# Splitting the next expert's weights into second buffers, two pieces a job over three jobs, in a mixture-of-experts loop on one core

## The chip, the cores and the metric

The kernel runs on one core of one Trainium2 chip. The metric is device time in microseconds (us); lower is better. The engines are named as in the profile: PE is TensorE (PEld its weight loads), DVE is VectorE, ACT is ScalarE, POOL is GpSimd, SP is SyncE, which issues most DMAs. Each engine runs its own instruction stream and waits for others on semaphores. A name with a q (ACTq) is the sequencer that feeds an engine: it executes branches and register work and hands out the instructions.

## The reference

Two stages. The first is a linear attention with decay over 32 pairs of batch and head:

```
for t in range(S):                                   # S = 768, head_dim 48
    cur = einsum('bhd,bhe->bhde', u * kt, vt)
    y[:, :, t] = einsum('bhd,bhde->bhe', rt, state + cur)
    state = w * state + einsum('bhd,bhe->bhde', kt, vt)
```

Its output, as 3072 tokens of 384 numbers, goes through a mixture of eight experts, one expert per token:

```
logits = x @ w_gate + modality_bias[modality_id]
e_idx, gate_w = argmax(logits), softmax(logits)[e_idx]
for e in range(8):
    h = maximum(x[e_idx == e] @ w1[e], 0.0)          # w1: 384 x 1024
    out[e_idx == e] = gate_w * (h @ w2[e])           # w2: 1024 x 384
```

## The kernel before, in words

**The stages.** Up to about 204 us of the profile the attention runs in 24 units of 128 tokens, and each unit's tokens are sent to rows of a buffer in memory sorted by expert. Beside the attention the first nine jobs of the first expert are worked off. A *job* is 128 rows of one expert. For this data three experts get tokens: 1569, 1354 and 149.

**The job table.** When the counts are known, DVE computes a table on the device (`jobs`) with a column per remaining job: the row to start from (ROW), a code (CODE) and the number of an expert to load (MORE). There are 17 such jobs here: 4 of the first expert, 11 of the second, 2 of the third. Job 0 is written out ahead of a hardware loop (`For_i`), whose 16 turns work off jobs 1 to 16. So the expert changes at job 4 and at job 15.

**One job.** `raise_` multiplies the job's tokens (`mxT`, held as a high and a low f16 half) by w1 into `phb`, in three groups of 4, 2 and 2 blocks of 128 columns (g0, g1, g2). ACT takes the relu of each group into `hh` (f16, the high half), DVE the rest into `hl`. `high_terms` multiplies `hh` by w2's high and low halves into `po`, `low_terms` multiplies `hl` by the high half; `low_terms` and `put` of a job stand at the top of the next turn. `put` has ACT scale `po` by the gate's factor `fac` into `otb`, and POOL send `otb` out by an indirect DMA. `take_in` has DVE copy the next job's tokens from `xn`, where a DMA has put them, to `mxT`, and their gates from `mn` to `mt`.

**The weights.** An expert's w1 and w2 lie as 6144 columns of 32-bit numbers per partition in `raw` after a DMA, and as f16 halves `whi` and `wlo` for the matmuls. Scaling and splitting goes by six pieces of 1024 columns: pieces 0 to 2 are w1, 3 to 5 are w2. Per piece ACT writes `whi` (L885: scale and round) and DVE `wlo` (L890: scaled value minus `whi`). Before that, ACT sums the squares of each piece (`norms`, L855), from which a power of two is derived as the scale `ws` with its inverse `winv`; `undo` puts the inverse into `wf`, which enters `fac`.

**What the code does before.** ACT, DVE and POOL load a job's code at the top of a turn, and branch on it. Bit 8, in the last job of an expert, runs `first_half` at the turn's end: pieces 0 to 2, straight into `whi` and `wlo`, once PE has read the old ones. Bit 4, in the first job of the next expert, runs `second_half` between `low_terms` and `put`: pieces 3 to 5, shared between ACT, DVE and POOL (L1357, L1358 and L1364 on POOL, L1360 on ACT, L1363 on DVE). Otherwise bits 1 and 2 run the norms of pieces 0 to 2 and 3 to 5, at the same place, two jobs and one job ahead of the change. MORE has SP load the expert after next into `raw` in the first job of an expert (`next_load`).

Of the kernel before, what the change touches and what calls it, by code (L numbers as in the profile page):

```python
# [35 lines left out]
GONE = 1000  # L36
NQ = 6
# [14 lines left out]
SP, ACT, AD = (mybir.EngineType.SP,), (mybir.EngineType.Activation,), (mybir.EngineType.Activation, mybir.EngineType.DVE, mybir.EngineType.Pool)  # L52
# [7 lines left out]
class _Kernel:  # L60
# [654 lines left out]
    def jobs(self):  # L715
# [34 lines left out]
        jb, cum, ol, nx = self.jb, self.cum, self.ol, self.nx  # L750
# [7 lines left out]
        v.tensor_copy(jc[:, 0:1], jb[:, 1:2])  # L758
        v.scalar_tensor_tensor(jc[:, 1:], act[:, 2:], 2.0, jb[:, 2 : E + 1], ALU.mult, ALU.max)
# [8 lines left out]
        v.tensor_add(ol[:, 1, 1:], cs, jb[:, 1 : E + 1])  # L768
        yield
        od, jr = new("od", [P, 2, E]), new("jr", [P, 2])  # L770
        v.tensor_sub(od, ol[:, :, 1:], ol[:, :, :E])
        yield
        v.scalar_tensor_tensor(od, cs.unsqueeze(1).to_broadcast([P, 2, E]), self.line, od, ALU.is_le, ALU.mult)
        csm = new("csm")
        v.scalar_tensor_tensor(csm, act[:, :E], float(-GONE), cs, ALU.mult, ALU.add)
        yield
        v.reduce_sum(jr, od, axis=AX.X)
        eq = new("eq", [P, 4, E])
        v.scalar_tensor_tensor(eq, csm.unsqueeze(1).to_broadcast([P, 4, E]), self.line, self.grid, ALU.subtract, ALU.is_equal)
# [4 lines left out]
        v.scalar_tensor_tensor(nx[:, : E - 1], eid[:, 1:], float(E), act[:, 1:E], ALU.add, ALU.mult)  # L784
        f, g = new("jf", [P, 4]), new("jg", [P, 4])
        v.reduce_sum(f, eq[:, :, 1:], axis=AX.X)
        v.reduce_sum(g, eq[:, :, 2:], axis=AX.X)
# [3 lines left out]

        last, now, soon, then = (slice(q, q + 1) for q in range(4))
        a, b = new("ja", [P, 1]), new("jbit", [P, 1])
        v.tensor_scalar(a, f[:, now], -1.0, 1.0, ALU.mult, ALU.add)
        v.scalar_tensor_tensor(b, f[:, last], 2.0, g[:, soon], ALU.add, ALU.mult)
        yield
        v.scalar_tensor_tensor(b, g[:, then], a, b, ALU.mult, ALU.add)
        mr = new("mr", [P, E - 1])  # L800
        v.tensor_mul(mr, eq[:, 1, 1:], nx[:, 1:])
        yield
        v.scalar_tensor_tensor(b, f[:, now], 4.0, b, ALU.mult, ALU.add)
        v.reduce_sum(field[:, MORE : MORE + 1], mr, axis=AX.X)
        yield
        v.scalar_tensor_tensor(field[:, CODE : CODE + 1], f[:, soon], 8.0, b, ALU.mult, ALU.add)
# [224 lines left out]
    def run(self):  # L1031
# [312 lines left out]
        whole = self.late.tile([P, 768], F32, name="scaled")  # L1344
        def first_half(code):
            with tc.If(code > 7):
                for q in range(NQ // 2):
                    self.split(q, 2 if q == 0 else 1)

        def second_half(code):  # L1350
            with tc.If(code % 8 > 3) as first:
                self.undo()
                self.split(NQ // 2)

                sl, sc = self.piece(NQ - 1, 0, 1)
                lo, hi = slice(sl.stop - 768, sl.stop), slice(sl.stop - 512, sl.stop)
                nc.gpsimd.tensor_tensor(whole, self.raw[:, lo], sc.to_broadcast([P, 768]), ALU.mult)  # L1357
                nc.gpsimd.tensor_tensor(self.whi[:, hi], self.raw[:, hi], sc.to_broadcast([P, 512]), ALU.mult)  # L1358
                mid = slice(sl.start - WQ, hi.start)
                nc.scalar.activation(self.whi[:, mid], self.raw[:, mid], AF.Copy, scale=sc)  # L1360
                self.fine(NQ - 2)
                rest = slice(sl.start, lo.start)
                nc.vector.scalar_tensor_tensor(self.wlo[:, rest], self.raw[:, rest], sc, self.whi[:, rest], ALU.mult, ALU.subtract)  # L1363
                nc.gpsimd.tensor_tensor(self.wlo[:, lo], whole, self.whi[:, lo], ALU.subtract)  # L1364
# [71 lines left out]
```

## Time and profile before

| | |
|---|---|
| median of 3 runs | 358.66 us (357.81 to 358.69) |
| the profiled execution's own time | 357.66 us |
| its span in the profile | 355.9 us, 15051 instructions |
| granted TensorE clock, mean | 0.977 |
| busy share of PE, DVE, ACT, POOL | 94%, 64%, 49%, 47% |
| length of an ordinary job in the loop | 7.94 us |
| the loop | jobs' first `phb` matmuls from 216.04 us on |

The profile gives one execution. A row of its timeline has the start in us, the length in us, the engine, the line of the program, the operation with output <- input by the program's names, the shape, how many instructions the row joins, and in brackets the time for which the engine stood idle ahead of it, with what ended that. A row of groups has busy us and mean ns of one behind the first bar, idle time behind the second.

### The profile page before, as it was taken

The numbers are of one execution on the slowest core, as the hardware profiler recorded it, in microseconds if no ns is written. First come the engines' busy times: TensorE is split into PE (matmuls) and PEld (weight loads), VectorE is DVE, ScalarE is ACT, GpSimd is POOL, SyncE is SP. The second block draws the span as 40 slices with busy tenths as digits, with TensorE's granted clock in tenths as the row PEclk, the third lists the DMA queues.
The fourth block names the chain that finished last, engine by engine and source line by source line (L and its number), as shares of the span: only waits on it lengthen the run. The fifth ranks groups of instructions, "written<-read, shape, count | busy, mean of one in ns | idle before, by whom it ended". The sixth has DMA issues, their size and how long they took to land. (4 is left out here: it accounts for less than half of the span.)

```text
span 355.9 us, 15051 instructions
## 1 busy us (share of the span) xinstructions
PE 334.4 (94%) x5415; PEld 267.7 (75%) x5415; DVE 227.7 (64%) x751; ACT 173.1 (49%) x457; POOL 168.3 (47%) x233
## 2 busy tenths in 40 slices
PE   7979999978999999999999999998999999999792
PEld 3657787868988797888877677776788888777671
DVE  6997999978895859596658732259423233334950
ACT  7469764865755577475532122255122222257620
POOL 8796777949736573345166511136111211111821
PEclk9999999995799999999999999999999999999998
DMA  6999899999937899763345641124822112112120
GB/s 181 263 200 196 204 196 217 310 311 224 235 114 191 179 220 300 174 136 99 81 120 166 225 69 44 44 64 177 229 66 44 44 50 61 44 31 58 22 57 5
DMA packets 60749, 50.29 MB, mean 141 GB/s; under 512 B 46872, under 2 KB 54311, under 8 KB 60448
## 3 DMA queue, kind: packets, MB, share of 16 engines
q1 hardware_dynamic: 57504, 40.21, 50.3%
q0 software_dynamic: 3200, 9.47, 8.0%
q8 instruction: 30, 0.49, 0.6%
q14 instruction: 15, 0.12, 0.1%
HBM read 28.39 MB, written 11.83 MB: 113 GB/s over the span
## 5 line engine op out<-in xcount | busy, mean ns | idle before, releaser
L944 PEld LDWEIGHTS <-whi 128*128 128x128 f16 x1248 | 73.5, 99 | 3.8 <-issue 0.8
L1018 PEld LDWEIGHTS <-hh 128*128 128x128 f16 x416 | 38.9, 98 | 29.5 <-issue 3.9
L944 PE MATMUL phb<-mxT,whi 128*128 128x128 f16 x768 | 50.7, 219 | 0.0
L369 ACT ACTIVATE dv<-kv,d 128x48 f32<-128x48 f32 x172 | 43.0, 324 | 4.2 <-DVE d L357 2.3
L944 PEld LDWEIGHTS <-wlo 128*128 128x128 f16 x624 | 38.4, 99 | 1.5 <-DVE wlo L890 1.5
L953 DVE SCALAR_TENSOR_TENSOR hl<-phb,hh 128x256 f16<-128x256 f32 (+1 forms) x48 | 24.2, 512 | 21.6 <-ACT hh L948 17.6
L336 POOL TENSOR_TENSOR rk<-rc,kc 128x512 f32<-128x512 f32 x20 | 25.9, 1297 | 25.2 <-DVE posi L582 10.9
L948 ACT ACTIVATE hh<-phb 128x256 f16<-128x256 f32 (+1 forms) x48 | 21.4, 454 | 33.7 <-PE L944 15.0
L324 POOL TENSOR_TENSOR rc<-ud,powr 128x512 f32<-128x512 f32 (+1 forms) x27 | 31.5, 1171 | 10.0 <-DMA ud<-in_pd 7.0
L1028 DVE TENSOR_SCALAR fac<-mt,wf 128x1 f32<-128x1 f32 x17 | 3.6, 212 | 49.9 <-ACT otb L904 43.1
L389 DVE TENSOR_TENSOR at<-psc,mask 128x512 f32<-128x512 f32 x48 | 31.6, 680 | 2.6 <-PE psc L383 2.6
L904 ACT ACTIVATE otb<-po,fac 128x384 f32<-128x384 f32 x16 | 9.2, 578 | 46.7 <-PE phb L944 38.9
L1023 PEld LDWEIGHTS <-hl 128*128 128x128 f16 x208 | 19.2, 98 | 16.3 <-issue 3.9
L944 PE MATMUL phb<-mxT,wlo 128*128 128x128 f16 x384 | 29.6, 219 | 1.2 <-DVE wlo L890 1.2
L1018 PE MATMUL po<-wlo,hh 128*128 128x384 f16 x136 | 28.0, 326 | 2.7 <-DVE wlo L890 2.6
L608 POOL DMA_INDIRECT rows<-row,posi x24 | 24.6, 1026 | 11.0 <-issue 3.7
L913 POOL TENSOR_TENSOR seenb<-otb,putb 128x1 int32<-128x1 int32 x16 | 5.0, 311 | 52.4 <-ACT otb L904 48.2
L890 DVE SCALAR_TENSOR_TENSOR wlo<-raw,ws,whi 128x1024 f16<-128x1024 f32 (+1 forms) x18 | 28.1, 1604 | 1.8 <-ACT whi L885 1.8
L944 PE MATMUL phs<-mxT,whi 128*128 128x128 f16 x432 | 28.4, 224 | 0.0
L420 PE MATMUL py<-kv,at 128*64 128x48 f32 x768 | 27.4, 225 | 0.9 <-issue 0.9
L383 PE MATMUL psc<-rc,kc 64*64 64x128 f32 (+1 forms) x768 | 27.8, 282 | 0.4 <-DVE kc L343 0.2
L1018 PE MATMUL po<-whi,hh 128*128 128x384 f16 x136 | 27.7, 326 | 0.1
(261 smaller groups left out, 670.7 us busy)
## 6 DMA issues: line engine op xcount, KB each, us to landing
ud<-in_pd SPq DMA_DIRECT2D x24, 384.0 KB, 7.4
kv<-in_pt SPq DMA_DIRECT2D x24, 384.0 KB, 6.3
raw<-in_w SPq DMA_DIRECT2D x12, 512.0 KB, 6.3
raw<-in_w SPq DMA_DIRECT2D x2, 1536.0 KB, 7.2
rows<-pad SPq DMA_DIRECT2D x10, 193.0 KB, 2.7
rows<-row,posi POOLq DMA_INDIRECT x24, 3.8
xT<-row SPq DMA_TRANSPOSE x23, 4.7
xn<-rows SPq DMA_TRANSPOSE x17, 3.9
```

Source lines behind the costliest of these rows:

```text
L324: nc.gpsimd.tensor_mul(u["rc"][:, s], u["rT"][:, s], self.powr[:, s])
L336: (eng or nc.gpsimd).tensor_mul(u["rk"], u["rc"], u["kc"])
L369: nc.scalar.activation(u["dv"][:, sl], u["v"][:, sl], AF.Copy, scale=u["d"][:, h : h + 1])
L383: nc.tensor.matmul(u["ps"][j][s, pr * P : (pr + 1) * P], u["kc"][r, pr, s], u["rc"][r, pr, :], start=True, stop=True)
L389: nc.vector.tensor_mul(u["at"][:, j * NPR : (j + 1) * NPR, :], u["ps"][j].rearrange("p (q t) -> p q t", q=NPR), self.mask.unsqueeze(1).to_ ...
L420: nc.tensor.matmul(py[t, sl], u["at"][:, j * NPR + pr, t], u["v"][:, sl], start=c == h == 0, stop=h == H - 1, skip_group_check=True)
L608: i = nc.gpsimd.indirect_dma_start(out=self.rows, out_offset=bass.IndirectOffsetOnAxis(ap=u["posi"][:, b : b + 1], axis=0), in_=u["row"][: ...
L890: self.nc.vector.scalar_tensor_tensor(self.wlo[:, sl], self.raw[:, sl], sc, self.whi[:, sl], ALU.mult, ALU.subtract)
L944: self.nc.tensor.matmul(ph[:, q * P : (q + 1) * P], w[:, c0 : c0 + P], self.xT[:, xq, t * P : (t + 1) * P], start=i == q == 0, stop=i == l ...
L948: self.nc.scalar.activation(self.hh[:, f0 : f0 + fb, t * P : (t + 1) * P], p3, AF.Relu)
L953: self.nc.vector.scalar_tensor_tensor(self.hl[:, f0 : f0 + fb, r], p3, 0.0, self.hh[:, f0 : f0 + fb, r], ALU.max, ALU.subtract)
L1018: self.nc.tensor.matmul(po[:, :DM], self.hh[:, f, t * P : (t + 1) * P], w[:, c0 : c0 + DM], start=n == q == f == 0, stop=False)
```

## The change

The pieces are no longer split into `whi` and `wlo` at the change. Two further f16 buffers, `whi2` and `wlo2`, take them, two pieces a job, in the jobs four, three and two ahead of the change (`split_beside`, by ACT and DVE alone). In the last job of an expert `swap(0)` copies w1's pieces, at the end of the turn; in the first job of the next one `swap(1)` copies w2's, behind `put`. Of each three pieces, DVE copies both halves, except for the low half of the first, which ACT copies. The norms come six and five jobs ahead, in place of two and one. The load into `raw` goes out in the last job of an expert, a job sooner, as `raw` is not needed any more at the change. POOL reads no code and branches on none.

Here the code is 4 for job 0, ahead of the loop; 8, 16, 32 (with the load) and 64 for jobs 1 to 4; 1, 2, 4, 8, 16, 32 and 64 for jobs 9 to 15.

```diff
-AD = (Activation, DVE, Pool)
+STEPS = 6
+AD = (Activation, DVE)
...
-        whole = self.late.tile([P, 768], F32, name="scaled")
-        def first_half(code):
-            with tc.If(code > 7):
-                for q in range(NQ // 2):
-                    self.split(q, 2 if q == 0 else 1)
-
-        def second_half(code):
-            with tc.If(code % 8 > 3) as first:
...
-            with first.Else():
...
+        half = NQ // 2
+        whi2, wlo2 = (self.late.tile([P, 2 * WC], F16, name=n) for n in ("whi2", "wlo2"))
+
+        def square(code):
+            with tc.If(code % 4 > 0):
+                with tc.If(code % 2 > 0):
+                    norms(*range(half))
+                with tc.If(code % 4 > 1):
+                    norms(*range(half, NQ))
+
+        def split_beside(q):
+            sl, sc = self.piece(q, 0, 1)
+            nc.scalar.activation(whi2[:, sl], self.raw[:, sl], AF.Copy, scale=sc)
+            nc.vector.scalar_tensor_tensor(wlo2[:, sl], self.raw[:, sl], sc, whi2[:, sl], ALU.mult, ALU.subtract)
+
+        def swap(h):
+            for q in range(half * h, half * h + half):
+                sl, _ = self.piece(q, 0, 1)
+                nc.vector.tensor_copy(self.whi[:, sl], whi2[:, sl])
+                (nc.vector.tensor_copy if q % half else nc.scalar.copy)(self.wlo[:, sl], wlo2[:, sl])
+
+        def ready(code):
+            with tc.If(code % 64 > 31):
+                swap(0)
+            with tc.If(code % 32 > 3):
+                for n in range(3):
+                    with tc.If(code % (8 << n) >= 4 << n):
+                        for q in (2 * n, 2 * n + 1):
+                            split_beside(q)
+
+        def change(code):
+            with tc.If(code > 63):
                 self.undo()
...
+                swap(1)
...
-        first_half(self.at(CODE, 0, 15, AD))
+        ready(self.at(CODE, 0, 2 << STEPS, AD))
         with tc.For_i(1, nj, 1, ...) as i, ...:
             self.turn(0, self.at(ROW, i, E * CAP, SP, 1), mn, xn)
-            code = self.at(CODE, i, 15, AD)
+            code = self.at(CODE, i, 2 << STEPS, AD)
             self.low_terms(po)
-            second_half(code)
+            square(code)
             self.put(po, 0, "b")
+            change(code)
             next_load()
             self.due(m2)
...
             take_in()
             self.high_terms(po)
-            first_half(code)
+            ready(code)
```

The rest of the diff is in `jobs` and `setup3`: other vector operations of the same kind and number for the new codes, and six small constants set on POOL. On ACT the loop has 141 rows in the program's order where it had 85, on DVE 126 where it had 66.

Two places in the order, both on ACT. First, ahead of the loop: `pha` is `phb` of job 0, the row with `hh` and the last `pha` is its third relu, and the rows with a tile name `whi` are behind a branch on job 0's code. Before:

```order
L948 ACTIVATE hh<-pha_4688 128x2x128
L821 TENSOR_LOAD tab
L1346 COMPARE_AND_BRANCH
L885 ACTIVATE whi<-raw,ws 128x512 x2
L885 ACTIVATE whi<-raw,ws 128x1024 x2
L1346 UNCONDITIONAL_BRANCH x2
L948 ACTIVATE hh<-pha_4709 128x2x128
```

Now (the end of it, with the pairs of pieces 2 and 3 and of 4 and 5; that of pieces 0 and 1 stands ahead of these rows with a branch of its own, and ahead of that the copy of the low half; lines are one less than before):

```order
L1355 ACTIVATE whi_4764<-raw,ws 128x1024 x2
L1369 UNCONDITIONAL_BRANCH x2
L1369 REGISTER_ALU
L1369 COMPARE_AND_BRANCH
L1355 ACTIVATE whi_4764<-raw,ws 128x1024 x2
L1369 UNCONDITIONAL_BRANCH x2
L1367 UNCONDITIONAL_BRANCH
L947 ACTIVATE hh<-pha_4712 128x2x128
```

In both the third relu stands behind the branches. Second, in the loop, from `put` to the relus. Before:

```order
L904 ACTIVATE otb_4851<-po,fac 128x384
L1374 UNCONDITIONAL_BRANCH
L948 ISA
L948 ACTIVATE hh<-phb_4868 128x4x128
L948 ISA
L948 ACTIVATE hh<-phb_4907 128x2x128
```

Now:

```order
L903 ACTIVATE otb_4865<-po,fac 128x384
L1374 COMPARE_AND_BRANCH
L1362 ISA
L1362 COPY wlo<-wlo_4765 128x1024
L1374 UNCONDITIONAL_BRANCH
L1374 REGISTER_ALU
L1374 UNCONDITIONAL_BRANCH
L947 ISA
L947 ACTIVATE hh<-phb_4890 128x4x128
```

The branch around the copy at the change has come between `otb` and the first relu.

More of the change, by code (lines that the diff above doesn't have):

```diff
@@ L51 @@
 ROW, CODE, MORE = range(3)
-SP, ACT, AD = (mybir.EngineType.SP,), (mybir.EngineType.Activation,), (mybir.EngineType.Activation, mybir.EngineType.DVE, mybir.EngineType.Pool)
+SP, ACT, AD = (mybir.EngineType.SP,), (mybir.EngineType.Activation,), (mybir.EngineType.Activation, mybir.EngineType.DVE)
 WQ = 2 * WC // NQ
@@ L768, in jobs @@
         v.tensor_add(ol[:, 1, 1:], cs, jb[:, 1 : E + 1])
+        v.scalar_tensor_tensor(ol[:, 2, 1:], act[:, 1:], float(-GONE), cum[:, 1:], ALU.mult, ALU.add)
+        v.tensor_copy(ol[:, 3, 1:], cs)
         yield
[L770 removed]
+        od, jr = new("od", [P, 5, E]), new("jr", [P, 5])
         v.tensor_sub(od, ol[:, :, 1:], ol[:, :, :E])
         yield
[L773 to L775 removed]
+        v.scalar_tensor_tensor(od, cs.unsqueeze(1).to_broadcast([P, 5, E]), self.line, od, ALU.is_le, ALU.mult)
         yield
         v.reduce_sum(jr, od, axis=AX.X)
[L778 to L779 removed]
         yield
@@ L782, in jobs @@
         v.tensor_scalar(past, jr[:, 1:2], self.line, float(E * CAP), ALU.is_le, ALU.mult)
[L784 to L787, printed above, removed]
+        one = [P, 1]
+        first, other = new("first", one), new("other", one)
+        v.tensor_scalar(first, jr[:, 3:4], self.line, None, ALU.is_equal)
+        v.tensor_scalar(other, jr[:, 3:4], 0.0, None, ALU.is_gt)
         yield
         v.scalar_tensor_tensor(field[:, ROW : ROW + 1], jr[:, 0:1], self.linep, past, ALU.add, ALU.max)
[L794 to L797, printed above, removed]
+        near, due, b = new("near", [P, STEPS]), new("dues", [P, STEPS]), new("jbit", [P, 1])
+        v.tensor_scalar(near, self.grid, jr[:, 2:3], first, ALU.is_gt, ALU.mult)
+        v.scalar_tensor_tensor(due, self.grid, jr[:, 2:3], near, ALU.is_equal, ALU.add)
         yield
-        v.scalar_tensor_tensor(b, g[:, then], a, b, ALU.mult, ALU.add)
-        mr = new("mr", [P, E - 1])
-        v.tensor_mul(mr, eq[:, 1, 1:], nx[:, 1:])
+        v.tensor_mul(field[:, MORE : MORE + 1], jr[:, 4:5], due[:, STEPS - 1 :])
+        v.tensor_scalar_mul(due[:, :2], due[:, :2], other)
         yield
-        v.scalar_tensor_tensor(b, f[:, now], 4.0, b, ALU.mult, ALU.add)
-        v.reduce_sum(field[:, MORE : MORE + 1], mr, axis=AX.X)
+        v.tensor_mul(due, due, self.bits)
+        v.tensor_mul(first, first, other)
         yield
-        v.scalar_tensor_tensor(field[:, CODE : CODE + 1], f[:, soon], 8.0, b, ALU.mult, ALU.add)
+        v.reduce_sum(b, due, axis=AX.X)
+        yield
+        v.scalar_tensor_tensor(field[:, CODE : CODE + 1], first, float(1 << STEPS), b, ALU.mult, ALU.add)
         yield
@@ L1343, in run @@
         norms = lambda *qs: [self.norm(junk, q) for q in qs]
-        whole = self.late.tile([P, 768], F32, name="scaled")
-        def first_half(code):
-            with tc.If(code > 7):
-                for q in range(NQ // 2):
-                    self.split(q, 2 if q == 0 else 1)
-        def second_half(code):
-            with tc.If(code % 8 > 3) as first:
-                self.undo()
[L1353 to L1364, printed above, removed]
-            with first.Else():
-                with tc.If(code % 4 > 0):
-                    with tc.If(code % 2 > 0):
-                        norms(*range(NQ // 2))
-                    with tc.If(code % 4 > 1):
-                        norms(*range(NQ // 2, NQ))
```

19 lines of the change are left out of this document (11 added, 8 removed).

## The prediction

> **What bounds the kernel now.** I read the page's busy shares first, then the table of stretches job by job, then the waits of the stage, then the single instructions around the stalls.
>
> ```profile
> PE 334.4 (94%) x5415; PEld 267.7 (75%) x5415; DVE 227.7 (64%) x751; ACT 173.1 (49%) x457; POOL 168.3 (47%) x233
> 231.94:239.88 7.94, 7.94 (x98) 6.39 (x97) 4.57 (x13) 4.77 (x8) 3.09 (x4) 1.00 0.20 48
> 239.88:250.27 10.39, 8.61 (x99) 6.20 (x97) 10.13 (x18) 4.81 (x7) 6.10 (x4) 1.00 0.54 182
> 330.01:340.78 10.77, 8.45 (x100) 6.20 (x98) 10.51 (x17) 4.70 (x7) 8.53 (x6) 1.00 0.09 22
> PE po L1018 <- DVE wlo L890: 2.6, 2, 1.9
> PEld L944 <- DVE wlo L890: 1.5, 2, 1.0
> PE phb L944 <- DVE wlo L890: 1.2, 2, 0.9
> ```
>
> The first row is the page's. Each stretch (span, length, then busy time of PE, PEld, DVE, ACT, POOL) runs from one job's first `phb` matmul to the next one's. In an ordinary job (231.94) PE is busy for all of 7.94 us: TensorE is the bound, and the others count only where PE stops for them. In the two jobs where the expert changes (job 4 at 239.88, job 15 at 330.01) the length is 10.39 and 10.77, so 2.45 and 2.83 us over 7.94, with DVE busy nearly throughout. The waits (total, times, longest) name DVE's L890, the weights' low halves.
>
> ```profile
> 238.43 5.13 DVE L890 SCALAR_TENSOR_TENSOR wlo<-raw,ws,whi 128x512 f16<-128x512 f32 x3
> 242.42 0.68 PE L944 MATMUL phb<-mxT,wlo 128*128 128x128 f16 x9 [0.87 <-DVE wlo L890]
> 246.07 1.27 DVE L890 SCALAR_TENSOR_TENSOR wlo<-raw,ws,whi 128x1024 f16<-128x1024 f32 x1
> 247.39 0.81 PE L1018 MATMUL po<-wlo,hh 128*128 128x384 f16 x4 [0.71 <-DVE wlo L890]
> 337.90 0.81 PE L1018 MATMUL po<-wlo,hh 128*128 128x384 f16 x4 [1.89 <-DVE wlo L890]
> L890 DVE SCALAR_TENSOR_TENSOR wlo<-raw,ws,whi 128x1024 f16<-128x1024 f32 x14 | 24.1, 1763 | 1.8 <-ACT whi L885 1.8
> L885 ACT ACTIVATE whi<-raw,ws 128x1024 f16<-128x1024 f32 x12 | 13.0, 1135 | 0.0
> ```
>
> A piece costs ACT 1.135 us. It costs DVE 1.27 where POOL splits nothing beside it, against a mean of 1.763. The new code has no POOL share, so I take 1.27. Below, t counts from a job's first `phb` matmul.
>
> **The change: what it removes.** The split within the change goes: 2.45 + 2.83 = 5.28 us. The norms go from jobs 13 and 14 to jobs 9 and 10 and leave a stall of 0.28 behind (rows below). Together 5.56 us that PE could win.
>
> **What it adds ahead of the loop.** The table's code for job 0 lies four jobs before the change, so pieces 0 and 1 are split there, and in program order this stands ahead of ACT's third relu `hh` and DVE's `hl` and `mxT`.
>
> ```profile
> L1346 ACTq COMPARE_BRANCH  x19: 58/99/101, 212.0 to 345.5; - x19
> 212.34 0.38 ACT L948 ACTIVATE hh<-pha 128x256 f16<-128x256 f32 x1 [0.56 <-PE pha L944]
> 212.76 0.42 DVE L953 SCALAR_TENSOR_TENSOR hl<-pha,hh 128x256 f16<-128x256 f32 x1 [0.20 <-ACT hh L948]
> 213.10 0.35 DVE L1335 COPY mxT<-xn 128x768 f16<-128x768 f16 x1
> 214.09 0.49 PE L1018 MATMUL po<-whi,hh 128*128 128x384 f16 x2
> 216.04 0.44 PE L944 MATMUL phb<-mxT,whi 128*128 128x128 f16 x5
> ```
>
> The first row is ACT's branch into an If (least/median/largest ns, first and last start): it enters this one at 212.0. ACT then skips the copies' If (about 0.5, below), passes two more branches (0.6) and splits from 213.13 to 215.30 (1.04 from start to start, then 1.135). It skips two more Ifs (0.65, the second partly overlapped) and runs the relu at 215.95 instead of 212.34, so PE's last two `po` pieces start at 216.38 instead of 214.09: 2.29. DVE's own two pieces end near 216.8, `hl` near 218.0 and `mxT` at 218.3, so `phb` starts at 218.4 instead of 216.04. The term is **+2.36**. No cover exists: PE has nothing else queued there.
>
> **What the extra Ifs cost.** The first four rows are an ordinary job's (`phb` at 231.94), the next four the sequencers', and the last is one of the waits.
>
> ```profile
> 232.38 0.58 ACT L904 ACTIVATE otb<-po,fac 128x384 f32<-128x384 f32 x1 [3.26 <-PE phb L944]
> 234.45 0.60 ACT L948 ACTIVATE hh<-phb 128x512 f16<-128x512 f32 x1 [1.50 <-PE L944]
> 235.98 1.14 PE L1018 MATMUL po<-whi,hh 128*128 128x384 f16 x6
> 237.70 0.16 DVE L1335 COPY mt<-mn 128x4 int16<-128x4 int16 x1
> L1346 ACTq EVENT_SEMAPHORE  x15: 17/17/17, 212.2 to 345.9; - x15
> L1378 ACTq FUSED_REGOPS  x16: 79/79/88, 221.3 to 346.0; - x16
> L1346 DVEq COMPARE_BRANCH  x19: 72/124/126, 212.4 to 345.9; - x19
> L821 ACTq TENSOR_LOAD <-tab x17: 273/279/524, 211.4 to 336.0; - x17
> ACT junk L855 <- PE po L1018: 1.8, 1, 1.8
> ```
>
> A skipped If on ACT lasts from 345.5 to 346.0, about 0.5, and its semaphore event waits for the engine's own last instruction, so nothing runs ahead through it. On DVE I take 0.64, the same times 124/99. The 1.79 us from a job's last relu to the norms in job 13 is one skipped If, the loop's return with the load of the code (then some 0.8, an estimate), and the entry into the norms (0.5). The loop has one more If per job on ACT and DVE, and one of them, `change`, now lies between `otb` and the first relu.
>
> ```profile
> 317.03 0.58 ACT L904 ACTIVATE otb<-po,fac 128x384 f32<-128x384 f32 x1 [0.71 <-PE L944]
> 317.51 0.86 ACT L948 ACTIVATE hh<-phb 128x512 f16<-128x512 f32 x2
> 318.16 1.15 PE L1018 MATMUL po<-whi,hh 128*128 128x384 f16 x6
> 324.65 0.56 ACT L904 ACTIVATE otb<-po,fac 128x384 f32<-128x384 f32 x1
> 325.11 0.94 ACT L948 ACTIVATE hh<-phb 128x512 f16<-128x512 f32 x2
> ```
>
> Before, the relu follows `otb` by 0.48 and `po` follows the relu by 0.65. With the If between, it is 0.97. In an ordinary job `otb` runs at t = 0.44, and the relu waits for PE to t = 2.51 anyway: nothing. `po` starts at t = 4.04 there, and that is the deadline.
>
> **Norm jobs 9 and 10.** Before, job 13 loses 0.28. The path has 0.33 more in `ready` and 0.49 more in `change`: **1.10**. Job 10 had a relu at t = 3.1 (325.11) and about 0.3 to spare; 0.82 later it loses **0.3** to 0.5. I take 0.3, as one of the Ifs is partly waited out.
>
> **Split jobs.** DVE's `mt` copy ends at t = 5.92 in an ordinary job; its copies' If is skipped by 6.56. ACT writes pieces 2 and 3 only after DVE has passed it (they share `whi2` with the copies). So ACT splits from 6.56 to 8.73, then the last If 0.47, return 0.81, the norms' If 0.47, 0.1 more: 10.6, or t = 2.66 of the next job for `otb`. The relu starts at 3.63, `po` at 4.28 against 4.04: **0.24** in job 2, and **0.2** in job 12. Where the job before has split too, DVE comes in late: its chain from `fac` to the `mt` copy takes 2.49 without any wait (the next fence), and `fac` would start near t = 4, so DVE passes the copies' If near 7.5, not 6.56. This delays ACT by 0.9 and `otb` to about 3.4: **1.0** in job 13. In job 3 pieces 4 and 5 have no such wait. For jobs 3, 4, 14 and 15 I take **0.1** each, bounds 0 and 0.9.
>
> ```profile
> 247.66 0.20 DVE L1028 TENSOR_SCALAR fac<-mt,wf 128x1 f32<-128x1 f32 x1
> 249.99 0.16 DVE L1335 COPY mt<-mn 128x4 int16<-128x4 int16 x1
> ```
>
> **The copies at the change.** No row shows an f16 copy of 1024 columns. Nearest is `mxT` above, 768 columns in 0.35 us; so 0.35 to 0.47 (in proportion), I take 0.41, or 1.7 us for five with overlapping starts. From t = 6.5 they end at 8.2, 0.25 into the next job, and low halves are read from 1.34: 0.1, inside the 0.1 above. At 0.47, or if DVE is late, up to 0.5. ACT's copy is one 1.135 us piece beside them. The half copied after `otb` is read from t = 4.04 and ends near 3.
>
> **Nothing for the rest.** The load of expert 4 goes out a job sooner; before, it made one wait.
>
> ```profile
> raw<-in_w SPq DMA_DIRECT2D x2, 1536.0 KB, 7.2
> DVE mxT L1335 <- DMA xn<-rows: 0.8, 1, 0.8
> ```
>
> Two halves of 7.2 us from t = 2 of job 3 end near t = 6 of job 4, and `xn` behind them on SP's queue near 7.0, needed at 7.5: cover 0.5; without it the price is that 0.8. POOL issues fewer instructions and PE never waits for it.
>
> **The sum.** 2.36 + 1.10 + 0.3 + 0.24 + 0.2 + 1.0 + 0.4 = 5.60 against 5.56 removed: +0.04 us. The profiled execution took 357.66 (span 355.9), so 357.7; it lies 1.0 under the median of the runs, 358.66, and against that the forecast is **358.7**.
>
> **The rivals.**
> *Hidden.* ACT and DVE get through norms and splits without touching PE, and only the pre-loop split and as much of the norms as before stay: -5.56 + 2.36 + 0.3 = -2.9, or 355.8. For it: PE is the bound and ACT is idle half the time. Against: `otb` already ended the idle time in job 13. It decides if `otb` runs before t = 2.4 after every split.
>
> *DVE falls behind.* Slower. From `fac` to `fac` a split job needs 2.49, two Ifs (1.0), 2 x 1.27 and the way back to `fac` (some 2.7): 8.8, more than 7.94. If that hits jobs 3, 4, 14 and 15 at 0.9 each instead of 0.1: +3.2, or 361.9. It decides where `fac` starts after t = 4 in two jobs running.
>
> *The raw load is late.* `xn` behind 3 MB costs 0.8, at both halves 1.6: 359.5 to 360.3. Only DVE's one wait above speaks for it.
>
> *Code no longer stays loaded.*
>
> ```profile
> q14 instruction: 15, 0.12, 0.1%
> mt<-rows SPq DMA_DIRECT2D x10, 1.0 KB, 2.4
> ```
>
> The page counts few instruction packets in the whole span, so the loop of before is not fetched anew at each turn. The loop grows on ACT from 85 to 141 rows of the program's order, on DVE from 66 to 126. If a turn had to fetch, at about the 2.4 us of a small transfer, `otb` would fall to t = 2.8, PE lose 0.4 in each of 16 jobs and more after splits: above 365. [...]
>
> **How the numbers follow.** Forecast 0.44 (range 357.0 to 360.2), hidden 0.22, DVE behind 0.22, late load 0.07, code fetched 0.05. A change under 0.3% (1.1 us) can't be told from none here. Faster is hidden and 0.05 of the forecast's spread: 0.27. Slower is DVE behind, late load, fetch and 0.05: 0.39. The same: 0.34. The range runs from 355.3, half a us below hidden, to 361.8, just short of DVE behind's full price; outside lie the fetches and the tails of those two.
>
> **What would show it.** Right: a first `phb` of the loop some 2.4 us later than 216.04 after the last `pha`; no `po` or `phb` waiting for L890 in jobs 4 and 15; stalls of about 1 us at `hh` in job 9 and job 13. Wrong: ACT's third relu before the split; job lengths of 7.94 after splits; more than 15 instruction packets on q14; `mxT` waiting for `xn`. The forecast hangs most on the waits of skipped Ifs: if an engine's sequencer does run ahead through them, most of the added terms vanish.

## The result and the profile after

The changed kernel takes 362.29 us (median of 6 runs, 360.82 to 366.18) where the kernel before takes 358.68 beside it (6 runs): the ratio on record is 1.0135, with a 95% interval of 1.0087 to 1.0183. All ratios here are those on record, from fast runs alone, and not quotients of the medians (1.010 here); one profile below, that of scale_earlier, is of a slow run. The kernel is slower, by 3.6 us between the medians. The forecast was 358.7 with a range up to 361.8, so the time lies outside.

The profiled execution, the fastest of the six, took 360.82 us with a span of 358.8, against 357.66 and 355.9 before. From the page and a table of stretches of the changed kernel (job 2, job 4, job 9, job 13 and job 15; columns as in the prediction, and behind them the granted clock, the share of the DMA engines and GB/s):

```profile
PE 334.0 (93%) x5415; PEld 266.4 (74%) x5415; DVE 229.6 (64%) x769; ACT 177.9 (50%) x461; POOL 158.4 (44%) x231
227.93:236.74 8.81, 8.11 (x100) 6.47 (x97) 4.83 (x13) 4.49 (x7) 1.57 (x3) 1.00 0.11 32
244.68:253.73 9.05, 8.12 (x99) 6.39 (x97) 4.38 (x18) 2.67 (x5) 1.60 (x4) 1.00 0.58 198
285.51:294.64 9.13, 8.12 (x99) 6.39 (x97) 2.44 (x11) 5.20 (x11) 1.36 (x3) 1.00 0.12 34
319.54:328.50 8.96, 8.10 (x99) 6.47 (x97) 4.83 (x13) 4.67 (x8) 1.58 (x3) 1.00 0.17 44
336.45:344.39 7.94, 7.94 (x98) 6.39 (x97) 4.39 (x18) 2.97 (x5) 1.36 (x3) 1.00 0.16 35
```

The splits have left the change: job 15 took 10.77 and takes 7.94, and PE waits for no split in the loop any more. In their place six other jobs (2, 4, 9, 10, 12, 13) take 8.29 to 9.13, and in the four shown (the first four stretches) DVE and ACT are busy for 57% of the time at most. They are not short of time; they come late.

The waits of the changed kernel from 211 us on (total, times, longest) name the new causes: the first relu, and a step of DVE's sequencer (line L1374 is the `change` If) for which PE itself waits in three jobs.

```profile
PEld L1017 <- ACT hh L947: 6.0, 5, 2.7
PE po L1017 <- ACT hh L947: 4.2, 3, 2.3
PE po L1017 <- DVEq L1374: 2.1, 3, 0.9
```

Ahead of the loop (timeline of the changed kernel: ACT, DVE, PE, then a stretch with the granted clock, third number from its end):

```profile
212.95 2.19 ACT L1355 ACTIVATE whi<-raw,ws 128x1024 f16<-128x1024 f32 x2 [1.55 <-DVEq L1365]
215.71 0.39 ACT L947 ACTIVATE hh<-pha 128x256 f16<-128x256 f32 x1 [0.58 <-ACTq L1369]
214.13 2.48 DVE L1356 SCALAR_TENSOR_TENSOR wlo<-raw,ws,whi 128x1024 f16<-128x1024 f32 x2 [1.96 <-ACT whi L1355]
216.15 0.66 PE L1017 MATMUL po<-whi,hh 128*128 128x384 f16 x2 [2.28 <-ACT hh L947]
217.68 2.47 PE L1022 MATMUL po<-whi,hl 128*128 128x384 f16 x8 [0.23 <-DVEq L1384]
219.99 1.50 PE L943 MATMUL phb<-mxT,whi 128*128 128x128 f16 x24
216.10:219.60 3.50, 3.22 (x11) 1.32 (x12) 1.28 (x4) 0.00 (x0) 0.27 (x1) 0.54 0.03 5
```

PE idles 2.28 us, as forecast. Two things behind it were not forecast. `low_terms`, the first work of PE inside the loop (L1384), starts only at 217.68, when DVE has entered the loop (0.23 us of idle time, ended by DVE's step at L1384). And the granted clock is 0.54 for 3.5 us (0.50 from 216.35 to 219.77), so that the eight matmuls of `low_terms`, 1.46 us before, take 2.47. The loop's first `phb` comes 13.89 us after the job table's matmul on PE, where it came 9.55 after it.

The stages, each from one profiled execution (us; a job's length runs to the next job's first `phb`). The experiments ran on two other chips (relu_first to three_mends on one, the rest on the other), on which the kernel before took 363 to 365 us. So their ratio is to the kernel before on the same chip beside them, and their lengths are best held against `changed_again`, the changed kernel on the second of these chips.

| kernel | table to loop | job 1 | 2 | 4 | 9 | 10 | 12 | 13 | 15 jobs | ratio (95%) |
|---|---|---|---|---|---|---|---|---|---|---|
| before | 9.55 | 7.95 | 7.95 | 10.39 | 7.94 | 7.95 | 7.95 | 8.23 | 124.74 | 1 |
| changed | 13.89 | 7.94 | 8.81 | 9.05 | 9.13 | 8.29 | 8.67 | 8.96 | 124.40 | 1.0135 (1.0087 to 1.0183) |
| changed_again | 14.05 | 8.39 | 9.43 | 9.09 | 9.78 | 8.27 | 9.32 | 8.96 | 127.25 | 1.0152 (1.0097 to 1.0207) |
| relu_first | 14.58 | 9.57 | 8.76 | 9.10 | 9.79 | 8.28 | 9.40 | 9.09 | 128.25 | 1.0205 (1.0125 to 1.0285) |
| splits_first | 12.62 | 11.84 | 11.26 | 8.08 | 9.55 | 8.10 | 12.26 | 12.08 | 143.17 | 1.0553 (1.0461 to 1.0644) |
| load_later | 14.06 | 8.38 | 9.42 | 8.03 | 9.78 | 8.28 | 9.33 | 8.96 | 126.35 | 1.0190 (1.0093 to 1.0288) |
| three_mends | 13.85 | 12.78 | 12.27 | 8.01 | 9.56 | 8.08 | 12.72 | 12.25 | 146.09 | 1.0647 (1.0586 to 1.0708) |
| job0_earlier | 11.47 | 8.04 | 9.47 | 8.86 | 9.78 | 8.28 | 9.32 | 8.97 | 126.88 | 1.0120 (1.0051 to 1.0188) |
| copies_early | 12.89 | 8.94 | 9.12 | 9.22 | 9.76 | 8.24 | 9.42 | 8.53 | 127.76 | 1.0121 (1.0046 to 1.0197) |
| own_codes | 13.00 | 8.84 | 8.28 | 7.99 | 8.51 | 7.95 | 8.50 | 8.09 | 122.72 | 0.9916 (0.9869 to 0.9962) |
| all_mended | 10.89 | 7.99 | 8.45 | 7.98 | 8.51 | 7.94 | 8.50 | 8.09 | 122.03 | 0.9929 (0.9881 to 0.9977) |
| scale_earlier | 10.89 | 8.04 | 8.44 | 7.98 | 8.51 | 7.94 | 8.49 | 8.06 | 121.85 | 0.9872 (0.9825 to 0.9919) |

Job 15 takes 10.77 before, and 7.94 to 8.23 in every other row.

### The profile page after: what moved, and what is told of

It reads as the page before. It is cut to its first block, busy times and chain, and to the rows that moved or that the text cites. A ratio compares the mean times of both kernels' runs of the same rounds, so it can differ in the third digit from the quotient of the medians.

```text
span 358.8 us, 15178 instructions
## 1 busy us (share of the span) xinstructions
PE 334.0 (93%) x5415; PEld 266.4 (74%) x5415; DVE 229.6 (64%) x769; ACT 177.9 (50%) x461; POOL 158.4 (44%) x231
## 3 DMA queue, kind: packets, MB, share of 16 engines
q0 software_dynamic: 3200, 9.47, 7.6%
## 5 line engine op out<-in xcount | busy, mean ns | idle before, releaser
L943 PEld LDWEIGHTS <-whi 128*128 128x128 f16 x1248 | 72.4, 98 | 3.6 <-issue 0.9
L912 POOL TENSOR_TENSOR seenb<-otb,putb 128x1 int32<-128x1 int32 x16 | 4.1, 258 | 65.4 <-ACTq L1374 61.8
L612 POOL DMA_INDIRECT rows<-row,posi x24 | 25.5, 1063 | 10.9 <-issue 3.9
L387 PEld LDWEIGHTS psc<-rc,kc 64*64 64x64 f32 (+1 forms) x768 | 22.1, 139 | 8.5 <-issue 3.9
L424 PEld LDWEIGHTS py<-kv,at 128*64 128x64 f32 x768 | 25.9, 142 | 2.6 <-issue 2.6
```

The costliest lines, as they stand in the source:

```text
L387: nc.tensor.matmul(u["ps"][j][s, pr * P : (pr + 1) * P], u["kc"][r, pr, s], u["rc"][r, pr, :], start=True, stop=True)
L424: nc.tensor.matmul(py[t, sl], u["at"][:, j * NPR + pr, t], u["v"][:, sl], start=c == h == 0, stop=h == H - 1, skip_group_check=True)
L612: i = nc.gpsimd.indirect_dma_start(out=self.rows, out_offset=bass.IndirectOffsetOnAxis(ap=u["posi"][:, b : b + 1], axis=0), in_=u["row"][: ...
L943: self.nc.tensor.matmul(ph[:, q * P : (q + 1) * P], w[:, c0 : c0 + P], self.xT[:, xq, t * P : (t + 1) * P], start=i == q == 0, stop=i == l ...
```

## The experiments

### The order ahead of the loop: relu_first

```diff
         self.high_terms(po)
-        ms.close()
-        self.ordered = False
...
         ready(self.at(CODE, 0, 2 << STEPS, AD))
+        ms.close()
+        self.ordered = False
```

(`ms` keeps the written order, so that the third relu now stands ahead of the branch.)

> Edit: the branch with job 0's two splits is put behind the third relu of job 0, in program order. Theory A (PE idles 2.28 us because the relu stands behind the split, and the clock that PE is granted then drops to half for about 3.5 us): the distance from job 0's first matmul to the loop's first falls from 12.28 us to about 8.0 (7.94 before the change), the granted clock stays near 1.0 there, and the time falls by about 4.2, to 358.1. Rival B (the split delays the start of the loop wherever it stands, because the loop's first turn waits for DVE and ACT): at most 1 us comes back, above 361. Rival C (the half clock belongs to the entry of the loop and not to the idle time): about 2.4 comes back, and the clock stays near 0.5 for 3.5 us.

The relu came on time, and nothing was won: 12.97 us from job 0's first matmul to the loop's first, against 12.28. The one stall has moved to the first matmul inside the loop (timeline of relu_first, and its stretch behind the stall):

```profile
223.53 2.72 PE L1022 MATMUL po<-whi,hl 128*128 128x384 f16 x8 [3.65 <-DVEq L1384]
223.50:226.90 3.40, 3.37 (x16) 2.01 (x17) 0.00 (x0) 0.38 (x1) 0.18 (x1) 0.50 0.31 61
```

L1384 is the loop. PE's first turn waits 3.65 us until DVE has entered the loop too, and in program order DVE's two splits stand ahead of that entry. Rival B holds: what costs is that the splits stand ahead of the loop's entry, not that they stand ahead of the relu. The half clock follows the idle time here as well (0.50 from 223.5 to 226.9), and goes on into job 1 (0.51 from 226.9 to 229.5; the job takes 9.57). Against rival C speaks splits_first, the next run: there the eight matmuls of `low_terms`, just behind the loop's entry (219.90), take 1.46 us, as in the kernel before, where the clock is 1.00.

### The order of the Ifs at a turn's end: splits_first

```diff
-            with tc.If(code % 64 > 31):
-                swap(0)
             with tc.If(code % 32 > 3):
...
+            with tc.If(code % 64 > 31):
+                swap(0)
```

> Edit: at the end of a turn the If of the splits stands ahead of the If of the copies. Theory A (ACT may write the second buffer only after DVE has passed the copies' If, DVE then ends its splits late, and PE's matmuls by w2 wait for DVE to pass the copies' If of the next job): ACT starts its splits in job 1 near t = 5.8 instead of 6.79, and the stalls at po in jobs 2, 12 and 13 (0.70, 0.57, 0.86) fall to under 0.3 each; jobs of 8.81, 8.67 and 8.96 become 7.95 to 8.2; time about 2.2 less, 360.1. Rival B (it is the number of Ifs that ACT and DVE step over, not their order): ACT's start moves by less than 0.3, the three jobs stay within 0.3 of 8.8, time 362.

ACT's splits came 0.5 us earlier (1.14 us behind the last relu in place of 1.67 in changed_again), between what the two theories said, and the kernel became 5.5% slower, which neither had. The timeline of splits_first, from job 1 to the start of job 2:

```profile
228.15 2.19 ACT L1355 ACTIVATE whi<-raw,ws 128x1024 f16<-128x1024 f32 x2 [1.14 <-DVEq L1367]
229.54 2.48 DVE L1356 SCALAR_TENSOR_TENSOR wlo<-raw,ws,whi 128x1024 f16<-128x1024 f32 x2 [1.73 <-ACT whi L1355]
233.04 0.45 PE L943 MATMUL phb<-mxT,whi 128*128 128x128 f16 x5 [3.69 <-DVEq L1370]
```

L1370 is here the copies' If, which is not taken in this job. PE's matmuls by w1 read a buffer that the If may write; they wait 3.69 us here, until DVE has stepped over it, and that is now behind DVE's splits. Jobs 1, 2, 11, 12 and 13 end in such a wait, of 2.3 to 3.8 us. Behind three of them PE is slow as well: behind 3.14 us the granted clock is 0.60 (244.3 to 247.0), and behind 3.83 and 2.82 the 24 `phb` matmuls take 2.53 and 1.85 us from start to start of the next group, where they take 1.34 at 1.00. The jobs lose 3.3 to 4.3 us each. I had looked for such a wait between DVE and ACT and overlooked it between DVE and PE. In the changed kernel the same condition stands in two places: for w1 at the turn's end, where no wait shows, and for w2 at `change` (the 2.1 us at L1374 above).

### The load a job later: load_later

```diff
-        v.scalar_tensor_tensor(ol[:, 4, 1 : E - 1], eid[:, 2:], float(E), act[:, 2:E], ...)
+        v.scalar_tensor_tensor(ol[:, 4, 1:E], eid[:, 1:], float(E), act[:, 1:E], ...)
...
-        v.tensor_mul(field[:, MORE : MORE + 1], jr[:, 4:5], due[:, STEPS - 1 :])
+        v.tensor_mul(field[:, MORE : MORE + 1], jr[:, 4:5], first)
```

> Edit: the load of the expert after next goes out in the first job of an expert, as before the change, and not in the last job of the one ahead. Theory A (in job 4 ACT's otb waits for the out DMA of the job before, which the load slows): otb in job 4 runs before t = 1.5 instead of 2.81, the job takes 7.95 to 8.2 instead of 9.05, time about 1.0 less, 361.3. Rival B (ACT's copy of 1.04 us between otb and the first relu is what PE waits for): job 4 stays at 8.7 to 9.05, time 362.3.

Theory A holds for the job: job 4 takes 8.03 against 9.09, and `otb` runs at 250.65, t = 0.96. The ratio, 1.0190 with an interval from 1.0093 on, does not show this microsecond. POOL's `putb` waits for the row of the job before to have left. In the changed kernel (first fence: the row leaves at 239.31) that wait is 6.38 us, in load_later (second fence) 1.78. The last row of the second fence is ACT's copy in load_later, which still stands ahead of the relu and costs nothing there; as it costs nothing in job 15 of the changed kernel, in which no load goes out.

```profile
239.31 1.87 POOL L913 DMA_INDIRECT out<-otb,putb  x1 [0.15 <-issue]
247.56 0.21 POOL L911 TENSOR_TENSOR putb<-ids,none 128x1 int32<-128x1 int32 x1 [6.38 <-DMA out<-otb,putb]
```

```profile
247.96 0.49 POOL L911 TENSOR_TENSOR putb<-ids,none 128x1 int32<-128x1 int32 x1 [1.78 <-DMA out<-otb,putb]
...
251.38 1.05 ACT L1362 COPY wlo<-wlo 128x1024 f16<-128x1024 f16 x1 [0.15 <-ACT otb L903]
```

The `otb` buffer is one, so the slow `out` DMA issued in job 3 holds up `otb` of job 4, behind which ACT's copy and the relu wait (the changed kernel, job 4 from 244.68):

```profile
247.49 0.58 ACT L903 ACTIVATE otb<-po,fac 128x384 f32<-128x384 f32 x1 [4.14 <-PE phb L943]
248.22 1.04 ACT L1362 COPY wlo<-wlo 128x1024 f16<-128x1024 f16 x1 [0.15 <-ACT otb L903]
249.17 1.14 ACT L947 ACTIVATE hh<-phb 128x512 f16<-128x512 f32 x3
```

The kernel before had the slow store too. Its load went out in job 4, and `otb` of job 5 (from 250.27) came just as late, but nothing stood between it and the relu, and job 5 took 7.95 (the kernel before):

```profile
252.95 0.58 ACT L904 ACTIVATE otb<-po,fac 128x384 f32<-128x384 f32 x1 [7.03 <-PE L944]
253.43 0.86 ACT L948 ACTIVATE hh<-phb 128x512 f16<-128x512 f32 x2
```

So the late `otb` (t = 2.81 here, 2.68 there) costs PE only together with ACT's copy behind it. The load a job sooner brought the two into the same job; rival B named the other half.

### The three together: three_mends

> Edit: the three edits together. Theory A (the three losses are separate): 4.2 + 2.2 + 1.0 less than the changed kernel, so about 355, which is 3.5 under the kernel before; stalls that stay are the norms in jobs 9 and 10, 1.5 together. Rival B (they hide one another, or the splits come in late again once PE does not stall ahead of the loop): 357.5 or more.

Neither theory had it. The ratio is 1.0647, as splits_first brings its own loss (jobs 1, 2, 12 and 13); rival B's bound of 357.5 holds, but not for its reasons. Only the part of load_later shows (job 4 at 8.01).

### Job 0's splits ahead of its matmuls: job0_earlier

```diff
         self.due(m2)
-        once = iter([lambda: self.scales("1")])
-        self.up("a", lambda: next(once, lambda: None)())
+        self.scales("1")
...
+        ready(self.at(CODE, 0, 2 << STEPS, AD))
+        self.up("a")
```

> Edit: the scale of the second expert's weights and the branch with job 0's two splits stand ahead of job 0's matmuls, where ACT and DVE wait for PE. Nothing else differs from the changed kernel. Theory A (PE enters the loop only when DVE has entered it, so DVE's two pieces ahead of the loop cost PE about 3.7 us of idle time and then some 1.6 at half the clock): from job 0's first matmul to the loop's first it takes 8.0 to 8.4 us in place of 12.28, the granted clock there stays at 1.0, and the ratio to the kernel before falls from 1.0135 by 4.0 us to about 1.002. Rival B (the two pieces only move the wait: job 0's first relu comes late): 10 us or more, ratio above 1.007.

From job 0's first matmul to the loop it takes 7.99, as before the change, and the clock stays at 1.00. But that first matmul comes 1.87 later behind the table (3.48 against 1.61), since PE waits there for DVE to step over the copies' If:

```profile
213.89 1.51 PE L943 MATMUL pha<-mxT,whi 128*128 128x128 f16 x24 [1.71 <-DVEq L1355]
```

So table to loop is 11.47, 2.6 less than in changed_again and not 4. Both theories are half right. The ratio, 1.0120, cannot be told from the changed kernel's.

### The copies' If where DVE waits anyway: copies_early

```diff
+                if g == 2:
+                    third()
                 low()
...
-            with tc.If(code % 64 > 31):
-                swap(0)
...
+        def copies(code):
+            with tc.If(code % 64 > 31):
+                swap(0)
...
+            self.up("b", lambda: next(beside, lambda: None)(), True, lambda: copies(code))
```

> Edit: the If with the copies of w1 stands ahead of DVE's third hl of the turn, where DVE waits anyway, instead of at the turn's end; the splits stay behind it at the end. Theory A (PE's matmuls by w1 and by w2 and ACT's splits wait until DVE has stepped over the copies' Ifs, taken or not, and DVE gets there late): ACT's splits in job 1 start near t = 5.9 instead of 6.79, DVE's end 0.9 earlier, the stalls at po in jobs 2, 12 and 13 (0.70, 0.57, 0.86) fall to under 0.3 each; about 2 us less, ratio 1.008. Rival B (DVE's own work is too long, so that starting 0.9 earlier only moves its wait): jobs 2, 12 and 13 stay at 8.6 or more, ratio 1.0135.

For job 1 this tells against my theory of ACT's wait. With the copies' If ahead of DVE's third `hl`, ACT starts its splits no sooner (timeline of copies_early, job 1; the last relu ends at 233.05):

```profile
232.67 0.38 ACT L947 ACTIVATE hh<-phb 128x256 f16<-128x256 f32 x1 [0.76 <-PE po L1019]
234.68 2.19 ACT L1357 ACTIVATE whi<-raw,ws 128x1024 f16<-128x1024 f32 x2 [1.63 <-DVEq L1369]
```

1.63 us against 1.67 in changed_again. In the changed kernel, where it is 1.67 too, DVE has passed the copies' If at 225.9, 0.9 ahead of the splits, and ACT's own steps fill the time: its relu ends at 225.11, it has stepped over the copies' If at 225.3, enters the next at 225.4, has stepped over the first pair's at 226.0, enters the second pair's, and splits from 226.78.

In job 12 it is otherwise. There DVE is late from the split of job 11, and ACT does wait for it to pass the copies' If, in changed_again (first row; L1365 is that If) and, for less long, in copies_early (second row; there it is L1374):

```profile
322.82 2.19 ACT L1355 ACTIVATE whi<-raw,ws 128x1024 f16<-128x1024 f32 x2 [2.77 <-DVEq L1365]
```

```profile
327.82 2.19 ACT L1357 ACTIVATE whi<-raw,ws 128x1024 f16<-128x1024 f32 x2 [2.15 <-DVEq L1374]
```

Job 13, which pays for it, falls from 8.96 to 8.53. Job 2 falls from 9.43 to 9.12, job 12 does not fall (9.42), and job 14 rises from 7.94 to 8.35, as the copies now stand ahead of its third `hl`, for which PE waits 0.25. The 15 jobs take 127.76 against 127.25. So the loop gains nothing, as rival B said, though not by its reason alone.

### A code for each engine: own_codes, and all together: all_mended, scale_earlier

```diff
-        def split_beside(q):
+        def wide_beside(q):
...
+        def fine_beside(q):
...
-                (nc.vector.tensor_copy if q % half else nc.scalar.copy)(self.wlo[:, sl], wlo2[:, sl])
...
+                nc.vector.tensor_copy(self.wlo[:, sl], wlo2[:, sl])
...
+        def ready(act, dve):
+            pairs(act, wide_beside)
+            pairs(dve, fine_beside)
...
-            code = self.at(CODE, i, 2 << STEPS, AD)
+            code, act = self.at(CODE, i, 2 << STEPS, DV), self.at(CODE, i, 2 << STEPS, ACT)
...
-            square(code)
+            square(act)
...
-            ready(code)
+            ready(act, code)
```

(`pairs` holds the Ifs of the splits as `ready` did; `change` and the copies now run on DVE alone. The edits of load_later and copies_early are in it too.)

> Edit: as copies_early; also the load goes out in the first job of an expert; and ACT and DVE each load a code of their own, so that ACT steps over the Ifs of norms and splits alone, DVE over those of copies and splits alone; all copies are DVE's. The work ahead of the loop stays as in the changed kernel. Theory A (job 9 pays for the Ifs that ACT steps over between the norms and the first relu, 0.8 of its 1.2): job 9 near 8.3 and job 10 near 7.95 (were 9.13 and 8.29), job 4 under 8.2 (was 9.05), jobs 2, 12, 13 under 8.2; ratio about 1.001. Rival B (the norms themselves, 3.5 us in ACT's stream, cost it): job 9 stays at 8.9 or more.

Most of the loop's loss is gone. Its 15 jobs take 122.72 us against 127.25, 2.0 less than the kernel before on the first chip, and the kernel is 0.8% faster than the one before. Of the 4.5 us job 4 has 1.1, as in load_later, and copies_early alone gave nothing; the rest comes with the codes and with the copies on DVE, which were not tried apart. ACT now starts its splits 1.07 us behind the last relu (own_codes, job 1), and in job 9 the relu follows `otb` by 0.48 again:

```profile
227.17 2.19 ACT L1357 ACTIVATE whi<-raw,ws 128x1024 f16<-128x1024 f32 x2 [1.07 <-DVEq L1372]
...
284.21 1.06 ACT L854 ACTIVATE junk<-raw 128x1024 f16<-128x1024 f32 x1 [1.44 <-PE po L1024]
...
288.43 0.58 ACT L903 ACTIVATE otb<-po,fac 128x384 f32<-128x384 f32 x1 [0.71 <-PE phb L943]
288.91 1.16 ACT L947 ACTIVATE hh<-phb 128x512 f16<-128x512 f32 x3
```

In the changed kernel the first norm started 2.18 behind the last relu and the relu 0.98 behind `otb` (job 9):

```profile
284.87 1.06 ACT L854 ACTIVATE junk<-raw 128x1024 f16<-128x1024 f32 x1 [2.18 <-PE po L1022]
...
289.10 0.58 ACT L903 ACTIVATE otb<-po,fac 128x384 f32<-128x384 f32 x1 [0.72 <-PE phb L943]
290.08 1.15 ACT L947 ACTIVATE hh<-phb 128x512 f16<-128x512 f32 x3 [0.40 <-PE phb L943]
```

Job 9 took 9.78 in changed_again and takes 8.51; 2, 12 and 13 get 0.8 to 1.2 shorter each. Rival B, which gave the norms the blame and job 9 at least 8.9, does not hold; norms and splits have the same durations as before (1.06 and 2.19 us, as the fences show). Not all of theory A does either: jobs 2, 9 and 12 stay 0.3 to 0.6 above an ordinary job, and jobs 3 and 14 take 8.28, as the copies now stand ahead of DVE's third `hl` and PE waits 0.17 for it.

> Edit: own_codes and job0_earlier together. Theory A (the losses add up): 8 us less than the changed kernel, ratio to the kernel before about 0.990; job lengths within 0.4 of the ordinary one all through the loop. Rival B (the copies at the change take the place of the splits as a stall, or DVE falls behind over three jobs with splits): ratio 0.997 or more.

`all_mended` joins the edits of own_codes and job0_earlier. It has table to loop at 10.89 and the loop at 122.03, both less than own_codes. Its ratio, 0.9929, is not to be told from own_codes': the executions of one kernel differ by more than these stages do (355.56 to 361.42 for all_mended). Neither theory's number is excluded.

scale_earlier moves the scale once more:

```diff
         self.s_due(8)
+        self.scales("1")
         fill(99)
...
         self.due(m2)
-        self.scales("1")
```

> Edit: as all_mended, and the scale of the second expert's weights is computed before the job table instead of behind it. Theory (ahead of the loop ACT starts job 0's two splits only when DVE has the scale, at 211.67, 3.5 us after the table's matmul, and job 0's relus stand behind them): from the table's matmul to the loop's first phb matmul it takes 9.6 to 9.9 us in place of 10.89 (before the change 9.55), and the ratio to the kernel before is about 0.990. Rival (the sequencers' branches and the load of the code set that start, and not the scale): 10.7 or more, ratio as all_mended's 0.993.

The rival holds: table to loop is 10.89 as in all_mended, and ACT starts job 0's splits 3.5 us behind the table's matmul whether the scale is ready or not (216.87 against 213.38; in all_mended 211.67 against 208.18; PE's first `po` comes 6.98 behind that matmul in both). The ratio of 0.9872 is the best measured, and the interval (0.9825 to 0.9919) puts this kernel clearly below the one before, by 0.8 to 1.8%; against all_mended the gain is not shown.

```profile
216.87 2.19 ACT L1347 ACTIVATE whi<-raw,ws 128x1024 f16<-128x1024 f32 x2 [1.04 <-issue]
219.71 1.15 ACT L947 ACTIVATE hh<-pha 128x512 f16<-128x512 f32 x3 [0.66 <-ACTq L1362]
```

### The changed kernel once more: changed_again

> The changed kernel as it is, beside the kernel before on the chip of this call, for the lengths of its jobs there. Theory (its losses lie in jobs 2, 4, 9, 10, 12 and 13 and ahead of the loop): these and no others are longer than an ordinary job; table to loop 13.9 us; ratio 1.009 to 1.018. Rival (the losses of single jobs depend on the phase in which DVE and ACT meet PE): jobs 2, 12 and 13 differ by more than 0.4 us from 8.81, 8.67 and 8.96.

The longer jobs are the same ones, with job 1 for the lower clock that reaches into it (0.86 from 221.4 to 225.0). But the rival has a point: job 2 is 9.43 against 8.81, job 12 9.32 against 8.67, and job 9 9.78 against 9.13, some 0.65 more each, while job 13 is the same. In ordinary jobs of this execution the second relu starts at t = 4.35, in the first one at 3.60:

```profile
273.22 0.38 ACT L947 ACTIVATE hh<-phb 128x256 f16<-128x256 f32 x1 [0.48 <-PE phb L943]
```

```profile
276.70 0.38 ACT L947 ACTIVATE hh<-phb 128x256 f16<-128x256 f32 x1 [1.24 <-PE po L1017]
```

(Job 7, from 269.62 in the changed kernel and from 272.35 in changed_again.) PE shows no idle time there, but its first six `po` matmuls take 1.24 us in place of 1.14, and the job 8.05 in place of 7.95. In PE's rows of all profiles from the two later chips they take 1.18 to 1.30 in most ordinary jobs, whatever the kernel, and 1.14 in all ordinary jobs of both profiles from the first chip. ACT begins its norms and splits that much later, and then it counts: the first norm of job 9 starts 0.64 ahead of the job's first `phb` in the changed kernel (284.87 and 285.51) and together with it in changed_again (288.44). Why the relu comes later there stays open. Part of the 363 to 365 us of the kernel before on those chips may come from it, but no profile of that kernel from there shows it.

## Why the prediction was wrong

**The sum's base and its removed part held.** The 2.45 and 2.83 us at the change are gone. The stall at the norms moved from job 13 to job 9.

**Ahead of the loop: 2.36 forecast, 4.34 measured.** The step that failed is "`phb` starts at 218.4". The start of the last `po` matmuls moved by 2.45, near the 2.29 forecast. But I let PE go on from there as before, with `low_terms` and then `phb` at their old distances. Instead `low_terms` had to wait for DVE to enter the loop: it starts 0.87 later behind those `po` matmuls than before (1.53 in place of 0.65). PE's idle time there is only 0.23, because the `po` matmuls themselves ran at the half clock; at the full clock it would have been some 0.9 with the same start, by an estimate from the 0.65 that they took before, as none of DVE's waits ahead of its entry is for PE in this trace (1.96 for ACT's `whi`, 0.73 at its own sequencer). From `low_terms` to `phb` it took 1.02 more, and that is the half clock's price (2.31 in place of 1.30). The granted clock was 1.00 through the 2.28 us of idle time and for 0.2 us behind it, 0.50 for the next 3.42, and 1.00 again from 219.77. The prediction weighed no fall of the clock.

**Split jobs: 0.24, 0.2 and 1.0 for jobs 2, 12 and 13, measured 0.87, 0.73 and 1.02.** The step that failed in all three is that `po` waits for the relu alone (in job 2 "the relu starts at 3.63, `po` at 4.28"). PE also waits in `po` until DVE has stepped over `change`, as that branch may write w2; I missed that it stands in PE's way. It shows in three jobs, with 0.57 in job 12 and the two here (the changed kernel, jobs 2 and 13):

```profile
231.84 1.21 ACT L947 ACTIVATE hh<-phb 128x512 f16<-128x512 f32 x3 [0.40 <-PE phb L943]
232.84 1.14 PE L1017 MATMUL po<-whi,hh 128*128 128x384 f16 x6 [0.70 <-DVEq L1374]
323.59 1.15 ACT L947 ACTIVATE hh<-phb 128x512 f16<-128x512 f32 x3 [0.40 <-PE phb L943]
324.61 1.14 PE L1017 MATMUL po<-whi,hh 128*128 128x384 f16 x6 [0.86 <-DVEq L1374]
```

`po` follows the relu by 1.00 and 1.02 here, where it followed by 0.65 before, so some 0.35 of each job's loss is DVE's step; the rest is the relu, which starts at t = 3.91 in job 2.

The chain ahead of the relu was half right. ACT's splits in the changed kernel (jobs 1 and 12):

```profile
226.78 2.19 ACT L1355 ACTIVATE whi<-raw,ws 128x1024 f16<-128x1024 f32 x2 [1.67 <-ACTq L1369]
318.55 2.19 ACT L1355 ACTIVATE whi<-raw,ws 128x1024 f16<-128x1024 f32 x2 [2.56 <-DVEq L1365]
```

In job 1 they start at t = 6.79, near the 6.56 forecast, but DVE's passing of the copies' If is not the reason: it comes 0.9 earlier, at 225.9, copies_early refutes it too, and ACT's own steps over the Ifs fill the time. In job 12 the wait that I worked out for DVE behind its own split is there: the `mt` copy ends at t = 7.43, where I had DVE pass the copies' If near 7.5, and ACT starts its splits at 7.68, 0.9 later than in job 1, as said. So for job 13 this step was right. Its 1.0 was met all the same by luck in part, as the relu came 0.3 sooner than forecast and DVE's step over `change` some 0.35 later. Behind all this, ACT and DVE spend 1.67 to 2.35 us between pieces of work (around the splits of job 1: ACT 1.67 ahead of them and 1.89 behind them, DVE 2.35 behind its own) while their sequencers step over Ifs, one behind the other, and return in the loop with the load of the code; own_codes takes some of them away, and the three jobs fall by 0.8 to 1.2. Jobs 3, 14 and 15 lost nothing (0.1 each forecast).

**Job 4: 0.1 forecast, 1.10 measured.** The copies cost what was said, 0.42 us each on DVE (0.41 forecast). The step that failed stands under "nothing for the rest": the load a job sooner was checked against `xn` alone. It was the `out` DMA of the job before that it slowed (POOL's wait for it 6.38 us, and 1.78 in load_later), and with it `otb`, in a job in which ACT's copy stands behind `otb`. load_later gives the 1.0 back.

**Norms: 1.10 and 0.3 forecast, 1.19 and 0.35 measured**, by the steps named: own_codes takes away two of ACT's Ifs on that way, and job 9 falls by 1.27 on its chip.

**What made up for some of it.** The end of the loop took 0.7 less (14.41 for 15.12, the wait of `low_terms` at the exit 1.01 in place of 1.63). Other runs with the changed order show either value (15.16 in changed_again, 14.53 in copies_early), so that is not the change's. The job table came 0.39 earlier.

Together, in us: 4.34 ahead of the loop and 5.22 in its jobs added (5.60 forecast for both), 5.56 removed, 1.1 given back: +2.9, the difference of the spans. The medians differ by 0.7 more, which no profile places. Of the rivals, "DVE falls behind" came nearest with 361.9, and part of its mechanism is there: in jobs 12 and 13 `fac` starts at t = 5.0 and 5.3, past the t = 4 in two jobs running that it named. But jobs 3, 14 and 15, which it charged 0.9 each, lost nothing, and job 4 lost for another reason: DVE did not stay behind (3.9 in job 14). "Code no longer stays loaded" did not show (16 packets on q14 in the whole span where there were 15); no run shows a fetch at a turn, and its price of 2.4 us was an estimate from a small transfer.

## What to carry to other kernels

Spreading conditional work over more turns of a hardware loop multiplies the branches. In the traces here an engine that steps over one gets past it only when its own last instruction has ended (in the changed kernel ACT at 231.5 in job 2, as `otb` ends at 231.44, and DVE at 318.3 in job 12, as the `mt` copy ends at 318.30). So give each engine only the branches that hold work of its own (with that, the copies on DVE and the load later, the 15 jobs took 122.72 us in place of 127.25). In this kernel, a branch that may write a buffer held up the readers of that buffer until the writing engine had passed it, though not taken: 0.57 to 0.86 us at `change`, 2.33 to 3.83 at the copies' If in splits_first. Do not place it behind that engine's longest work (5.5% in splits_first); to place it where the engine is early gained nothing by itself (copies_early, 127.76 us for 127.25). Before a load is moved, look at every transfer that shares the time with it, the stores too, and ask which buffer they hold (here that of `otb`: job 4 took 9.09 us, and 8.03 with the load a job later).

## What the hardware showed that I had not expected

An idle time of PE of 2.28 us was followed by 3.5 us at a granted clock of 0.54; one of 1.89 us (job 15 before) and ones of 0.70, 0.93 and 1.01 (jobs 2, 4 and 9 of the changed kernel) were not (1.00). One of 3.69 (splits_first, ahead of job 2) was not either (1.00), while one of 3.14 ahead of job 3 was (0.60). In own_codes 1.65 and 0.71 shortly after each other were followed by 0.63, but 1.95 and 0.78 in splits_first by eight matmuls in 1.46 us, as at 1.00. So in these runs the length alone does not decide it, and what does stays open.

PE's first turn of the loop waited 3.65 us for DVE to enter the loop (relu_first: its last matmuls ahead of it start at 219.40, `low_terms` at 223.53, released by DVE's step at the loop's line).

An indirect store of one job kept its buffer for some 8 us beside a load of 3 MB (issued at 239.31, the next index written at 247.56), and in the kernel before for 6.7 (246.34 and 253.02); the median to landing is 2.6 us on the page of before:

```profile
out<-otb,putb POOLq DMA_INDIRECT x16, 2.6
```
